# Multiplying 128 tail tokens in the last joint layer instead of in the sweep of batch 1

## The chip, the cores and the metric

One Trainium2 chip, one core. The metric is the device time of one execution of the program, in microseconds. Engines are named as in the profile: PE (TensorE matmul), PEld (its weight load), DVE (VectorE), ACT (ScalarE), POOL (GpSimd), SP (SyncE, which issues most transfers).

## What is computed

Attention over 4 batches, 12 heads, 448 tokens and head size 64, with RMS-normalised q and k, then two feed-forward blocks over all 4 x 448 = 1792 tokens of width 768. In short:

```
x = softmax(scale * norm(q) @ norm(k).T) @ v            # (4, 12, 448, 64) -> (1792, 768)
x = sigmoid(x @ w_gate) * (x @ w_val) @ w_out           # 768 -> 1536 -> 768
h = relu(x @ w_in); out = (h * h) @ w_out2              # 768 -> 2048 -> 768
```

q, k, v and the output are float32, the weights float64. The kernel holds each operand as two fp32r parts (a rounded high part and the rest), and one product of two operands is three matmuls: high x high, high x low and low x high.

## The kernel before

The work has three stages on PE. In `sweep(0)` and `sweep(1)` the four layers of batch 0 and of batch 1 are multiplied one after the other (gate and value, output of the first block, the third layer with relu and square, the last layer). In `joint()` batches 2 and 3 go through the four layers together.

While PE multiplies batch 0, the attention of batch 1 is woven between its matmuls, and while it multiplies batch 1, the attention of batches 2 and 3. Each `yield` in `sweep` is a step. At each step the main loop at the end of the program takes the next slots of the list `slots_of` and emits their work. In sweep 1 there are 204 steps and 202 slots, and one pair of heads takes 16 or 17 slots: scores (`s_mm2`, 4 matmuls into one `att` tile), their maximum (`s_max2`, DVE), the exponentials (`s_exp2`, ACT), the transposes of the result (`c_mm2`, 7 into one `att` tile), the high part of them (`c_hi`, ACT) and the rest (`c_lo`, DVE), the weighted sum of values (`pv_mm2`, 7 matmuls `att<-parts,vs`), and for the next pair the transposes of q and k (`do_a2`, 8 matmuls `att<-ident,qk`) with their split (`a_hi` on ACT, `a_lo` on DVE). There are two `att` tiles in PSUM, used in turn, so each of these steps on PE needs what the last but one left there to have been read. On PE the order in sweep 1 and in `joint` is that of the program (`fixed`). On ACT, DVE, POOL and SP a scheduler sets the order.

Weights come as blocks of 128x768. `next_block` hands out the next and splits the one that is three blocks ahead into a high part (ACT, `wsp<-wraw`) and the rest (DVE). In the last layer of a sweep a block holds 2 of 16 groups of 128 inner rows for half of the 768 columns, and each chunk of 128 tokens takes 6 matmuls of 384 columns per block. 448 tokens are three chunks of 128 and a tail of 64. The third-layer results of the tail of batch 0 are kept in SBUF (`rtail`) in two parts, those of batch 1 join them, and sweep 1 multiplies four chunks: the joined tail `rt` and three of batch 1 (`rb`).

In `joint` every layer is in seven-product form: a product of 2x2 blocks takes seven products in place of eight, with sums and differences of blocks made beforehand (weights in DRAM by accumulating transfers, tokens by DVE in `make`). In its last layer the 896 tokens of batches 2 and 3 are seven chunks of 128. Six of them are in the form (two halves of 384 tokens), and the seventh, `plain`, is multiplied in the plain way by `thin`. Each of the seven products `n` runs over four groups `g`. In each, one weight block is split and 3 x 6 matmuls follow, and `make(n + 1, g)` prepares the tokens of the next product. `thin` adds 6 matmuls in each group of products 0, 1, 4 and 5, and in product 4 a block of weights of its own.

Of the kernel before, what the change touches and what calls it, by code (L numbers as in the profile page):

```python
# [8 lines left out]
F32 = mybir.dt.float32  # L9
# [8 lines left out]
def attention_moe_moe2_kernel(  # L18
# [14 lines left out]
    nc = tc.nc  # L33
# [94 lines left out]
    for both in (((None, (0, 0)),), ((None, (1, 0)),), ((0, None),), ((1, None),), ((2, None), (None, (0, 1))),  # L128
                 ((None, (1, 1)),), ((3, None),)):
# [466 lines left out]
    rtail = {}  # L596

# [146 lines left out]
    def joint():  # L744
# [130 lines left out]
        ra = one.tile([128, 13, 2 * N], F32, tag="hr", name="r")  # L875
        rb = one.tile([128, 3 * 2 * N], F32, tag="pt", name="r")
        plain = one.tile([128, K2, 2, 128], F32R, tag="rt", name="plain")

        def r_of(k):
            return ra[:, k] if k < 13 else rb[:, (k - 13) * 2 * N:(k - 12) * 2 * N]  # L880

        for m2 in range(K2 // 2):
            for m, n, o, sign in seven(yp):
# [4 lines left out]
                if n == 1:  # L888
                    src = r_of(k)[:, 768:896]
                    nc.scalar.copy(out=plain[:, k, 0], in_=src)  # L890
                    nc.vector.tensor_tensor(
                        out=plain[:, k, 1], in0=src, in1=plain[:, k, 0].bitcast(F32), op=ALU.subtract)
        beat_on(30)
        yield
        row0 = 2 * N
        rest = one.tile([128, 7, 2, 384], F32, tag="xy0", name="rest")
        fsum = [rest[:, 3 + i] for i in range(4)]
        dsum = [two.tile([128, 2, 384], F32, tag="qk", name="dsum"), one.tile([128, 2, 384], F32, tag="vs", name="dsum")]
        keep = [rest[:, i // 2, i % 2] for i in range(6)]
        base, third = keep[0:3], keep[3:6]  # L900

        def pairs_of(k, c0, g):
            return [r_of(4 * g + 2 * i + k)[:, c0:c0 + 384] for i in range(2)]

        def vector2(dst, g, in0, in1, op):
            for i in range(2):
                held(nc.vector.tensor_tensor(
                    out=dst[:, i], in0=in0[i] if isinstance(in0, list) else in0[:, i],
                    in1=in1[i] if isinstance(in1, list) else in1[:, i], op=op))

        bufs = [[], []]
        for tag, pool, n in (("raw64", raw_p, 1), ("raw64", raw_p, 1), ("raw64", raw_p, 1), ("qs", one, 1)):
            rp = pool.tile([128, 2, 2, 384], F32R, tag=tag, name="rp")
            bufs[0].append((rp[:, 0], rp[:, 1]))
        xy = one.tile([128, 3, 2, 2, 384], F32R, tag="xy1", name="rp")
        bufs[1] = [(xy[:, i, 0], xy[:, i, 1]) for i in range(3)] + [
            tuple(p_p.tile([128, 2, 384], F32R, tag="p", name="rp") for _ in range(2))]

        def make(n, g):
            dst = bufs[n % 2][g]  # L920
            a11, a12 = pairs_of(0, 0, g), pairs_of(1, 0, g)
            a21, a22 = pairs_of(0, 384, g), pairs_of(1, 384, g)
            if n in (0, 1, 6):
                src = (a11, a12, None, None, None, None, a22)[n]
            elif n == 2:
                vector2(fsum[g], g, a21, a22, ALU.subtract)
                src = fsum[g]
            elif n == 3:
                vector2(fsum[g], g, a11, fsum[g], ALU.subtract)
                src = fsum[g]  # L930
            elif n == 4:
                src = dsum[g % 2]
                vector2(src, g, a11, a21, ALU.subtract)
            else:
                vector2(fsum[g], g, a12, fsum[g], ALU.subtract)
                src = fsum[g]
            if isinstance(src, list):
                for i in range(2):
                    nc.scalar.copy(out=dst[0][:, i], in_=src[i])
                    nc.vector.tensor_tensor(  # L940
                        out=dst[1][:, i], in0=src[i], in1=dst[0][:, i].bitcast(F32), op=ALU.subtract)
            else:
                nc.scalar.copy(out=dst[0], in_=src)
                nc.vector.tensor_tensor(out=dst[1], in0=src, in1=dst[0].bitcast(F32), op=ALU.subtract)
            return dst

        def put(chunk, hf, fn):
            ob = tmp("ob")[:, :384]
            fn(ob)
            row = row0 + 128 * chunk  # L950
            nc.sync.dma_start(out=out[row:row + 128, hf * 384:(hf + 1) * 384], in_=ob)

        xs = [acc_tile()[:, :384] for _ in range(3)]
        y0, y1 = att_tile(), att_tile()
        ys = [y0[:, 0, :384], y0[:, 1, :384], y1[:, 0, :384]]
        zs = [y1[:, 1, :384], acc_tile()[:, :384]]
        bank = [xs, xs, ys, xs, xs, ys, xs]
        ready = {(0, g): make(0, g) for g in range(K4 // 2)}

        def thin(z, wb, g, odd, start, stop):  # L960
            for kk in range(2):
                k = 2 * (2 * g + kk) + odd
                wh, wl = wb[:, 0, kk], wb[:, 1, kk]
                rh, rl = plain[:, k, 0], plain[:, k, 1]
                mm(out=z, lhsT=rh, rhs=wh, start=start and g == 0 and kk == 0, stop=False)
                mm(out=z, lhsT=rh, rhs=wl, start=False, stop=False)
                mm(out=z, lhsT=rl, rhs=wh, start=False, stop=stop and g == K4 // 2 - 1 and kk == 1)

        def end(n, p):
# [8 lines left out]
            elif n == 4:  # L978
                put(p + 3, 1, lambda ob: nc.vector.tensor_tensor(out=ob, in0=third[p], in1=o, op=ALU.subtract))
# [3 lines left out]
            elif n == 6:  # L983
                put(p + 3, 0, lambda ob: nc.vector.tensor_tensor(out=ob, in0=o, in1=base[p], op=ALU.add))

        for n in range(7):
            for g in range(K4 // 2):
# [4 lines left out]
                for p in range(3):  # L992
                    o = bank[n][p]
                    for kk in range(2):
                        rh, rl = (op[i][:, kk, 128 * p:128 * (p + 1)] for i in range(2))
# [5 lines left out]
                    if g == K4 // 2 - 1 and (n != 5 or p > 0):  # L1001
                        if n == 5 and p == 1:
                            end(n, 0)
                        end(n, p)
                if n in (0, 1):
                    thin(zs[0], wb, g, n, n == 0, n == 1)
                elif n == 4:
# [3 lines left out]
            if n in (1, 5):  # L1011
                z = zs[n // 5]
                put(6, n // 5, lambda ob: nc.scalar.copy(out=ob, in_=z))
        yield

    def sweep(s):
# [59 lines left out]
        if s % 2 == 0:  # L1076
            rtail[0] = one.tile([128, 2, K2, 128], F32R, tag="rt", name="rt")
            parts = [(rb, 0, 0, NM), (rtail[0], 0, NM, TAIL)]
        else:
            parts = [(rtail[0], TAIL, 0, TAIL), (rb, 0, TAIL, NM)]  # L1080
# [401 lines left out]
```

## Time and profile before

| | us |
|---|---|
| median of 3 runs (1230.23 to 1231.26) | 1230.28 |
| the profiled execution | 1230.38 |
| its span, from the first to the last instruction | 1228.2 |
| PE busy in the span | 1216.1 |
| PEld busy | 1072.2 |
| DVE busy | 981.8 |
| ACT busy | 797.2 |
| POOL busy | 237.1 |

The profiled execution took 2.2 us more than its span. PE idle is the difference of span and busy time, 12.1 us. The granted clock of PE is full in every slice of the span.

### The profile page before, as it was taken

The numbers are of one execution on the slowest core, as the hardware profiler recorded it, in microseconds if no ns is written. First come the engines' busy times: TensorE is split into PE (matmuls) and PEld (weight loads), VectorE is DVE, ScalarE is ACT, GpSimd is POOL, SyncE is SP. The second block draws the span as 40 slices with busy tenths as digits, with TensorE's granted clock in tenths as the row PEclk, the third lists the DMA queues.
The fourth block names the chain that finished last, engine by engine and source line by source line (L and its number), as shares of the span: only waits on it lengthen the run. The fifth ranks groups of instructions, "written<-read, shape, count | busy, mean of one in ns | idle before, by whom it ended". The sixth has DMA issues, their size and how long they took to land.

```text
span 1228.2 us, 19243 instructions
## 1 busy us (share of the span) xinstructions
PE 1216.1 (99%) x6572; PEld 1072.2 (87%) x6572; DVE 981.8 (80%) x1548; ACT 797.2 (65%) x1611; POOL 237.1 (19%) x248
## 2 busy tenths in 40 slices
PE   8999999999999999999999999999999999999998
PEld 5548878878889988989898999999999999999998
DVE  6888988778975788888788777878888658778793
ACT  6787888667765778876798766765657324335461
POOL 3312222211120113233222220022111112120000
PEclk9999999999999999999999999999999999999999
DMA  5557998888896667787778643597768767675443
GB/s 140 134 162 243 313 293 262 275 256 249 251 316 184 159 161 165 181 177 186 166 183 174 153 93 108 149 210 207 194 179 193 182 166 196 173 194 154 135 148 103
DMA packets 207121, 232.30 MB, mean 189 GB/s; under 512 B 84784, under 2 KB 186288, under 8 KB 207024
## 3 DMA queue, kind: packets, MB, share of 16 engines
q1 hardware_dynamic: 181840, 179.49, 50.4%
q0 software_dynamic: 23296, 51.13, 19.5%
q8 instruction: 52, 0.85, 0.3%
q10 hardware_dynamic: 1888, 0.46, 0.2%
q14 instruction: 45, 0.37, 0.1%
HBM read 192.48 MB, written 81.00 MB: 223 GB/s over the span
## 4 chain that ended last, share of the span: by engine, by line
PE 94%; ACT 2%; DVE 1%; DMA 1%; SPq 1%; issue 1%; ACTq 0%; DVEq 0%
PE acc L578 60%; PE att L578 21%; PE att L583 3%; PE att L303 3%; PE att L357 2%; PE acc L357 1%; PE att L339 1%; PE acc L583 1%; PE acc L339 1%; ACT p L321 1%; DMA ks<-ks 0%; ACT p L470 0%; DMA wraw<-w 0%; PE att L362 0%; DMA qk<-in_k_dram 0%
## 5 line engine op out<-in xcount | busy, mean ns | idle before, releaser
L205 ACT CAST wsp<-wraw 128x768 fp32r<-128x768 f32 x254 | 212.4, 837 | 187.1 <-PE att L578 86.9
L578 PE MATMUL acc<-xy,wsp 128*128 128x448 f32 x1422 | 313.5, 371 | 0.8 <-ACT rl L1093 0.6
L206 DVE TENSOR_TENSOR wsp<-wraw,wsp 128x768 fp32r<-128x768 f32 x254 | 243.3, 959 | 78.0 <-ACT wsp L205 75.1
L578 PEld LDWEIGHTS acc<-xy,wsp 128*128 128x128 f32 x1422 | 261.3, 188 | 31.2 <-issue 6.8
L578 PE MATMUL att<-parts,wsp 128*128 128x448 f32 x828 | 175.8, 365 | 0.0
L578 PEld LDWEIGHTS att<-parts,wsp 128*128 128x128 f32 x828 | 155.5, 188 | 12.3
L578 PE MATMUL acc<-parts,wsp 128*128 128x448 f32 x567 | 122.0, 365 | 0.0
L273 POOL TENSOR_TENSOR ms<-ms,mhalf 112x16 f32<-112x16 f32 (+1 forms) x25 | 79.8, 3195 | 182.8 <-DVE ms L272 182.8
L578 PEld LDWEIGHTS acc<-parts,wsp 128*128 128x128 f32 x567 | 106.4, 188 | 8.4
L578 PE MATMUL acc<-wsp,rb 128*128 128x384 f32 x576 | 108.7, 338 | 0.0
L578 PEld LDWEIGHTS acc<-wsp,rb 128*128 128x128 f32 x576 | 99.8, 188 | 2.3 <-issue 2.0
L578 PE MATMUL acc<-hb,wsp 128*128 128x448 f32 x432 | 95.3, 371 | 0.0
L578 PEld LDWEIGHTS acc<-hb,wsp 128*128 128x128 f32 x432 | 79.3, 188 | 9.4 <-issue 2.7
L177 ACT ACTIVATE wraw<-raw 128x768 f32<-128x768 f32 x67 | 61.1, 917 | 31.2 <-DVE wsp L206 17.9
L192 POOL DMA_DIRECT2D w<-wraw x67 | 37.1, 554 | 219.8 <-DVE wraw L185 195.0
L470 ACT ACTIVATE p<-att,nm 112x448 f32<-112x448 f32 x96 | 60.1, 631 | 17.7 <-DVE nm L459 16.7
L321 ACT ACTIVATE p<-att,nm 112x448 f32<-112x448 f32 x88 | 55.3, 638 | 18.2 <-DVE nm L309 16.5
L185 DVE SCALAR_TENSOR_TENSOR wraw<-wraw,raw 128x768 int32<-128x768 int32 x67 | 63.9, 956 | 1.0
L578 PE MATMUL acc<-wsp,rp 128*128 128x384 f32 x360 | 64.5, 334 | 0.0
L578 PEld LDWEIGHTS acc<-wsp,rp 128*128 128x128 f32 x360 | 62.6, 188 | 0.0
L309 DVE TENSOR_REDUCE nm<-att 112x2 f32<-112x896 f32 x48 | 51.9, 1083 | 8.2 <-PE att L303 8.0
L609 POOL DMA_DIRECT2D wt<-w x32 | 26.6, 909 | 145.2 <-DMA wt<-wt 102.6
(224 smaller groups left out, 2050.8 us busy)
## 6 DMA issues: line engine op xcount, KB each, us to landing
wraw<-w SPq DMA_DIRECT2D x68, 384.0 KB, 3.5
w<-wraw POOLq DMA_DIRECT2D x67, 384.0 KB, 6.1
wraw<-w SPq DMA_DIRECT2D x113, 192.0 KB, 2.9
raw<-in_moe_w_out_dram SPq DMA_DIRECT2D x22, 768.0 KB, 6.3
raw<-in_moe_w_in_dram SPq DMA_DIRECT2D x16, 768.0 KB, 6.2
raw<-in_moe_w_gate_dram SPq DMA_DIRECT2D x12, 768.0 KB, 7.1
raw<-in_moe_w_val_dram SPq DMA_DIRECT2D x12, 768.0 KB, 7.1
ws<-w POOLq DMA_DIRECT2D x48, 192.0 KB, 4.7
```

Of the source, the lines that this page charges most:

```text
L177: size = nc.scalar.activation(out=t, in_=hi.bitcast(F32), func=AF.Prelu, scale=2.0 ** -112, alpha=2.0 ** 32)
L185: nc.vector.scalar_tensor_tensor(out=ti, in0=ti, scalar=3, in1=hi, op0=ALU.logical_shift_left, op1=ALU.bitwise_or)
L192: nc.gpsimd.dma_start(out=w32[i], in_=wraw[i])
L205: nc.scalar.copy(out=sp[:, 0], in_=t)
L206: nc.vector.tensor_tensor(out=sp[:, 1], in0=t, in1=sp[:, 0].bitcast(F32), op=ALU.subtract)
L273: nc.gpsimd.tensor_tensor(out=ms, in0=ms, in1=mhalf[:QR, 0:ms.shape[1]], op=ALU.pow)
L309: nc.vector.tensor_reduce(out=nm, in_=st["s", c][:QR, :, :S], axis=AX.X, op=ALU.max, negate=True)
L321: nc.scalar.activation(out=p[:, e], in_=ps[:QR, e, :S], func=AF.Exp, bias=nm[:, e:e + 1], scale=st["rq"][:, c, e:e + 1] if "rq" in st else ...
L357: nc.tensor.matmul(out=o[e * D:(e + 1) * D], lhsT=v[:, kc, e], rhs=pt[:, (NF + 1) * e + kc if kc < NF else NF], start=(kc == 0), stop=(kc ...
L470: nc.scalar.activation(out=p[:, i * S:(i + 1) * S], in_=ps[:QR, i, :S], func=AF.Exp, bias=nm[:, i:i + 1], accum_out=su[:, c, e:e + 1])
L578: m = latest[0] = nc.tensor.matmul(**kw)
L583: m = nc.tensor.transpose(*a)
```

## The change

Sweep 1 no longer multiplies the joined tail. Both sweeps keep the square of their 64 tail tokens as plain float32 in `rtail`; at the end of the third layer of sweep 1 the whole of it (128 x 2048 floats, 1 MB) is written to a tensor `tails` in DRAM. In `joint`, where the third-layer results of batches 2 and 3 are held in `ra` and `rb`, each row gets 1024 columns in place of 896, and two transfers put `tails` into the last 128. So the last joint layer has 8 chunks, all in seven-product form: two halves of 512 tokens, 4 x 6 matmuls per group in each of the seven products. `thin`, `plain` and the extra weight blocks of product 4 are gone. `make` works on 1024 columns in one instruction where two of 384 stood. The buffers of that stage are laid out anew. In sweep 1 the last layer has the same number of steps, now of 6 matmuls each (before 9, 9 and 6), and from step 156 on a slot comes one step later (`at_step`). The parts of batch 2 and 3 (`x_part`) are now attached to slots.

```diff
-    for both in (..., ((2, None), (None, (0, 1))), ((None, (1, 1)),), ((3, None),)):
+    for both in (..., ((2, None),), ((None, (1, 1)),), ((3, None),)):
...
+    tails = dram_p.tile([128, K2 * 128], F32, tag="tails", name="tails")
...
-        ra = one.tile([128, 13, 2 * N], F32, tag="hr", name="r")
-        rb = one.tile([128, 3 * 2 * N], F32, tag="pt", name="r")
-        plain = one.tile([128, K2, 2, 128], F32R, tag="rt", name="plain")
+        ra = one.tile([128, 12, 1024], F32, tag="hr", name="r")
+        rb = one.tile([128, 4, 1024], F32, tag="rt", name="r")
+        held(nc.sync.dma_start(out=ra[:, :, 2 * N:], in_=from_tails[:, 0:12]))
+        held(nc.sync.dma_start(out=rb[:, :, 2 * N:], in_=from_tails[:, 12:16]))
...
+            hi, lo = room[n % 2][g]
+            a11, a12 = pair_of(0, 0, g), pair_of(1, 0, g)
+            a21, a22 = pair_of(0, 512, g), pair_of(1, 512, g)
...
+                src = dsum if n == 4 else fsum[g]
+                first, second = {2: (a21, a22), 3: (a11, src), 4: (a11, a21), 5: (a12, src)}[n]
+                held(nc.vector.tensor_tensor(out=src, in0=first, in1=second, op=ALU.subtract))
+            nc.scalar.copy(out=hi, in_=src)
+            nc.vector.tensor_tensor(out=lo, in0=src, in1=hi.bitcast(F32), op=ALU.subtract)
...
-                for p in range(3):
+                for p in range(4):
...
-                if n in (0, 1):
-                    thin(zs[0], wb, g, n, n == 0, n == 1)
-                elif n == 4:
-                    thin(zs[1], block(), g, 0, True, False)
-                elif n == 5:
-                    thin(zs[1], wb, g, 1, False, True)
... (sweep)
-                for dst, d0, c0, cn in parts:
-                    low.tensor_tensor(...)
+                low.tensor_tensor(
+                    out=rb[:, 1, m], in0=r2[:, c0:c0 + NM], in1=rb[:, 0, m].bitcast(F32), op=ALU.subtract)
...
-            chunks = [(rtail.pop(0), 0, t0 - TAIL)] + chunks
+            nc.sync.dma_start(out=tails, in_=rtail.pop(0).rearrange("p k n -> p (k n)"))
...
-                        if s == 1 and (c, kk) in ((1, 0), (2, 1)):
+                        if s == 1 and (c, kk) in ((0, 1), (1, 1)):
... (main loop)
+    def at_step(i, total):
+        i += 1
+        if i <= 156:
+            return i + i * 0 // 156
+        return 156 + 0 + (i - 156) * (total - 156 - 0) // 47
```

On PE at the start of the last layer of sweep 1, from the first scores there to those that follow two steps of attention later, this stood before (`rt` is the joined tail, `rb` are the chunks of batch 1, `ks,qs` scores, `ident,p` transposes, `ident,qk` the transposes of `do_a2`, `parts,vs` weighted sums):

```order
L578 MATMUL att<-ks,qs 112x448 x4
L583 MATMUL att<-ident,p 128x112 x7
L578 MATMUL acc<-wsp,rb 128x384 x6
L578 MATMUL acc<-wsp,rt 128x384 x6
L578 MATMUL acc<-wsp,rb 128x384 x3
L583 MATMUL att<-ident,qk 128x112 x8
L578 MATMUL acc<-wsp,rb 128x384 x9
L578 MATMUL att<-parts,vs 128x448 x7
L578 MATMUL acc<-wsp,rb 128x384 x6
L578 MATMUL acc<-wsp,rt 128x384 x6
L578 MATMUL acc<-wsp,rb 128x384 x3
L578 MATMUL att<-ks,qs 112x448 x4
```

and this stands there now:

```order
L577 MATMUL att<-ks,qs 112x448 x4
L582 MATMUL att<-ident,p 128x112 x7
L577 MATMUL acc<-wsp,rb 128x384 x12
L582 MATMUL att<-ident,qk 128x112 x8
L577 MATMUL acc<-wsp,rb 128x384 x6
L577 MATMUL att<-parts,vs 128x448 x7
L577 MATMUL acc<-wsp,rb 128x384 x12
L577 MATMUL att<-ks,qs 112x448 x4
```

The attention on PE is the same, and 15, 9 and 15 matmuls of the layer between its pieces have become 12, 6 and 12. On ACT, a little later in the same layer, from the copies of one `x_part` to those of the next, this stood before (`p` are exponentials, two for one pair of score tiles, `parts<-att` with L491 and L494 the high part of the transposes):

```order
L651 CAST parts<-xwhole 128x448 x2
L470 ACTIVATE p,su<-att,nm 112x448 x2
L491 CAST parts<-att 128x3x224
L494 CAST parts<-att 64x112 x2
L205 CAST wsp<-wraw 128x768
L651 CAST parts<-xwhole 128x448 x2
```

and this stands there now:

```order
L651 CAST parts<-xwhole 128x448 x2
L204 CAST wsp<-wraw 128x768
L490 CAST parts<-att 128x3x224
L493 CAST parts<-att 64x112 x2
L469 ACTIVATE p,su<-att,nm 112x448 x2
L651 CAST parts<-xwhole 128x448 x2
```

The exponentials have moved behind the three copies of the transposes, which come later on PE than the scores that the exponentials read.

## Rows read from the trace of the kernel before

**Rows 1.** Page, part 4: the chain that ended last, by engine.
```profile
PE 94%; ACT 2%; DVE 1%; DMA 1%; SPq 1%; issue 1%; ACTq 0%; DVEq 0%
```

**Rows 2.** Windows, all engines: stretch, length, busy time and instructions, clock, DMA.
```profile
560.00:687.50 127.50, 126.68 (x702) 114.14 (x701) 107.00 (x186) 103.21 (x240) 31.48 (x28) 1.00 0.75 177
687.50:782.50 95.00, 94.65 (x572) 91.28 (x572) 73.42 (x123) 62.34 (x140) 13.82 (x10) 1.00 0.41 107
782.50:1120.30 337.80, 337.80 (x1670) 313.05 (x1669) 266.78 (x397) 166.81 (x289) 61.75 (x75) 1.00 0.75 189
1120.30:1228.20 107.90, 104.22 (x602) 103.89 (x600) 77.31 (x122) 45.45 (x68) 0.82 (x1) 1.00 0.43 130
```

**Rows 3.** Groups of instructions by form, PE: busy us, mean ns, idle before.
```profile
L578 PE MATMUL acc<-wsp,rt 128*128 128x384 f32 x96 | 19.8, 341 | 0.0
L578 PE MATMUL att<-wsp,plain 128*128 128x384 f32 x48 | 9.6, 334 | 0.0
```

**Rows 4.** Timeline, PE, last joint layer: start us, length us, instructions.
```profile
1123.48 1.20 PE L578 MATMUL att<-wsp,plain 128*128 128x384 f32 x6
1124.52 3.28 PE L578 MATMUL acc<-wsp,rp 128*128 128x384 f32 x18
```

**Rows 5.** Timeline, last layer of sweep 1, first pair of heads there.
```profile
691.47 0.83 PE L583 MATMUL att<-ident,p 112*128 112x112 f32 x7
692.08 1.29 PE L578 MATMUL acc<-wsp,rb 128*128 128x384 f32 x6
...
692.96 0.51 ACT L494 CAST parts<-att 64x112 fp32r<-64x112 f32 x2
...
693.49 0.64 ACT L470 ACTIVATE p<-att,nm 112x448 f32<-112x448 f32 x1
...
694.63 0.20 ACT L470 ACTIVATION_READ_ACCUMULATOR p<-att,nm 112x1 f32 x1
...
694.88 0.98 PE L583 MATMUL att<-ident,qk 112*128 112x112 f32 x8
...
700.24 0.63 DVE L437 TENSOR_TENSOR ks<-att,ks 64x448 fp32r<-64x448 f32 x1
...
701.34 0.99 PE L578 MATMUL att<-ks,qs 128*112 128x448 f32 x4
```

**Rows 6.** Timeline, the same layer, second pair of heads.
```profile
717.19 0.62 DVE L536 TENSOR_TENSOR xwhole<-xwhole,att 128x448 f32<-128x448 f32 x1
...
718.10 0.84 PE L583 MATMUL att<-ident,p 112*128 112x112 f32 x7
...
719.64 4.57 POOL L273 TENSOR_TENSOR ms<-ms,mhalf 112x16 f32<-112x16 f32 x1 [10.57 <-DVE ms L272]
...
722.20 0.56 DVE L503 TENSOR_TENSOR parts<-att,parts 64x112 fp32r<-64x112 f32 x2
...
723.76 0.83 PE L583 MATMUL att<-ident,p 112*128 112x112 f32 x7
...
728.09 0.99 PE L583 MATMUL att<-ident,qk 112*128 112x112 f32 x8 [0.35 <-ACT p L470]
```

**Rows 7.** Timeline, the same layer, weighted sum of the second pair.
```profile
746.97 1.73 PE L578 MATMUL att<-parts,vs 128*128 128x448 f32 x7
...
747.18 0.56 DVE L503 TENSOR_TENSOR parts<-att,parts 64x112 fp32r<-64x112 f32 x2
```

**Rows 8.** Windows, products 2 and 3 of the last joint layer with the start of 4.
```profile
1153.60:1187.00 33.40, 33.40 (x195) 33.40 (x194) 30.91 (x49) 18.73 (x26) 0.00 (x0) 1.00 0.45 145
```

**Rows 9.** Groups by form, DVE, 687.5 to 782.5: split of a weight block.
```profile
L206 DVE TENSOR_TENSOR wsp<-wraw,wsp 128x768 fp32r<-128x768 f32 x16 | 15.3, 954 | 3.2 <-ACT wsp L205 3.0
```

**Rows 10.** Page, part 6: transfers, KB each, us to landing.
```profile
raw<-in_moe_w_out_dram SPq DMA_DIRECT2D x22, 768.0 KB, 6.3
```

More of the change, by code (lines that the diff above doesn't have):

```diff
@@ L897, in joint @@
[L897 to L917, printed above, removed]
+        xy0 = one.tile([128, 5, 1024], F32R, tag="xy0", name="rp")
@@ new lines, in joint @@
+        xy1 = one.tile([128, 5, 1024], F32R, tag="xy1", name="rp")
+        pt = one.tile([128, 3, 1024], F32R, tag="pt", name="rp")
+        raw = [raw_p.tile([128, 1536], F32R, tag="raw64", name="rp")[:, :1024] for _ in range(3)]
+        kqs = [two.tile([128, 1024], F32, tag="kq", name="sums") for _ in range(2)]
+        qst = one.tile([128, 1024], F32, tag="qs", name="sums")
+        qks = [two.tile([128, 1024], F32, tag="qk", name="sums") for _ in range(2)]
+        vst = one.tile([128, 2, 512], F32, tag="vs", name="keep")
@@ new lines, in by_k @@
+        def by_k(t):
+            return t.rearrange("p (k n) -> p k n", k=2)
+        room = [
+            [(pt[:, 0], pt[:, 1]), (pt[:, 2], raw[0]), (raw[1], raw[2]), (xy0[:, 4], xy1[:, 4])],
+            [(t[:, i], t[:, i + 1]) for t in (xy1, xy0) for i in (0, 2)]]
+        room = [[(by_k(a), by_k(b)) for a, b in half_] for half_ in room]
+        fsum = [by_k(t) for t in (kqs[0], kqs[1], qks[0], qst)]
+        dsum = by_k(qks[1])
+        pkeep = [p_p.tile([128, 2, 384], F32, tag="p", name="keep") for _ in range(3)]
@@ L919, in make, with pair_of @@
+        keep = [t[:, i] for t in pkeep for i in range(2)] + [vst[:, i, :384] for i in range(2)]
+        base, third = keep[0:4], keep[4:8]
+        def pair_of(k, c0, g):
+            t, k0 = (ra, 4 * g + k) if g < 3 else (rb, k)
+            return t[:, k0:k0 + 3:2, c0:c0 + 512]
         def make(n, g):
-            dst = bufs[n % 2][g]
-            a11, a12 = pairs_of(0, 0, g), pairs_of(1, 0, g)
-            a21, a22 = pairs_of(0, 384, g), pairs_of(1, 384, g)
+            hi, lo = room[n % 2][g]
+            a11, a12 = pair_of(0, 0, g), pair_of(1, 0, g)
+            a21, a22 = pair_of(0, 512, g), pair_of(1, 512, g)
@@ L949, in put @@
             fn(ob)
-            row = row0 + 128 * chunk
+            row = 2 * N + 128 * chunk if chunk < 7 else N - TAIL
             nc.sync.dma_start(out=out[row:row + 128, hf * 384:(hf + 1) * 384], in_=ob)
[L953 to L956, printed above, removed]
+        xs = [acc_tile()[:, :384] for _ in range(4)]
+        ys = [t[:, i, :384] for t in (att_tile(), att_tile()) for i in range(2)]
         bank = [xs, xs, ys, xs, xs, ys, xs]
         ready = {(0, g): make(0, g) for g in range(K4 // 2)}
[L960 to L967, printed above, removed]
         def end(n, p):
@@ L978, in end @@
             elif n == 4:
-                put(p + 3, 1, lambda ob: nc.vector.tensor_tensor(out=ob, in0=third[p], in1=o, op=ALU.subtract))
+                put(p + 4, 1, lambda ob: nc.vector.tensor_tensor(out=ob, in0=third[p], in1=o, op=ALU.subtract))
                 nc.vector.tensor_tensor(out=base[p], in0=base[p], in1=o, op=ALU.add)
@@ L983, in end @@
             elif n == 6:
-                put(p + 3, 0, lambda ob: nc.vector.tensor_tensor(out=ob, in0=o, in1=base[p], op=ALU.add))
+                put(p + 4, 0, lambda ob: nc.vector.tensor_tensor(out=ob, in0=o, in1=base[p], op=ALU.add))
         for n in range(7):
@@ L1000, in joint @@
                         mm(out=o, lhsT=rl, rhs=wh, start=False, stop=g == K4 // 2 - 1 and kk == 1)
[L1001 to L1004, printed above, removed]
-                if n in (0, 1):
-                    thin(zs[0], wb, g, n, n == 0, n == 1)
-                elif n == 4:
-                    thin(zs[1], block(), g, 0, True, False)
-                elif n == 5:
-                    thin(zs[1], wb, g, 1, False, True)
-            if n in (1, 5):
-                z = zs[n // 5]
-                put(6, n // 5, lambda ob: nc.scalar.copy(out=ob, in_=z))
+                    if g == K4 // 2 - 1:
+                        if n != 5:
+                            end(n, p)
+                        elif p % 2:
+                            end(n, p - 1)
+                            end(n, p)
         yield
@@ L1425, in attention_moe_moe2_kernel @@
         total, done = len(slots), 0
-        extra = steps_of_1() if s == 1 else {}
+        extra = steps_of_1(slots) if s == 1 else {}
         for i, _ in enumerate(sweep(s)):
@@ L1436, in attention_moe_moe2_kernel @@
                 fn(*args)
[L1437 removed]
+            want = min(total, at_step(i, total) if s == 1 else (i + 1) * total // 66)
             while done < want:
```

67 lines of the change are left out of this document (19 added, 48 removed).

## The prediction

> **What bounds the kernel now.** The chain that ended last comes first: 94% of it is PE [rows 1]. So nearly all of the time is matmuls issued one after the other, and a change pays by the matmuls that it removes, less the waits that it makes on PE. The busy time by stretch says where such waits could come up [rows 2]. In the joint layers PE is busy for all of the 337.80 us, and in the last layer of sweep 1 (687.5 to 782.5) for 94.65 of 95.00 us. What differs is how close the others are. In that last layer DVE is busy for 73.42 us, 77%, and ACT for 62.34; in the layers ahead of it, with the same attention between their matmuls, DVE has 107.00 of 127.50 us, 84%. These shares are only averages: what PE waits for in such a layer are chains from PE over DVE and ACT back to PE, and whether they end in time is read from single places of the timeline, below.
>
> **Matmuls.** The tail chunk took 96 matmuls in sweep 1 [rows 3], and `thin` another 96 in the joint layer (two banks, of which the rows show the first; 2 halves x 16 groups x 3). The joint layer had 7 products x 4 groups x 18 = 504 besides, and now has 7 x 4 x 24 = 672. So 96 go in sweep 1, and 672 - 504 - 96 = 72 are added in the joint layer: 24 fewer in all. Six matmuls of 384 columns follow each other in 1124.52 - 1123.48 = 1.04 us [rows 4], 0.1733 us each. That is -16.64 us in sweep 1 and +12.48 us in the joint layer, together -4.16 us.
>
> **The waits in sweep 1.** The last layer of sweep 1 keeps its attention, and has 288 matmuls between its pieces where 384 stood. PE's work there falls to 94.65 - 16.64 = 78.0 us, DVE's stays at about 73 us: 94% if PE never waited. For each piece of attention on PE I take the time from its start back to the end of the chain that it needs, which is its slack, and set against it the matmuls that leave the stretch.
>
> *Two `att` tiles, exponentials.* After the transposes that start at 691.47 ACT makes their high part (until 693.47) and then the exponentials of the scores before them, the last of which is read out by 694.83; the transposes of q and k start at 694.88 [rows 5]. From the start of the transposes the chain is 3.36 us long, and PE has 0.61 us of transposes (691.47 to 692.08) and 15 matmuls, 2.60 us. It arrives with almost nothing to spare. With 12 matmuls PE needs 2.69 us and waits 0.67 us. The order of ACT now puts the exponentials behind the copies before the next pair's first scores too, where they stood ahead, with again 12 matmuls in front, and the second `ident,qk` gets 12 in place of 18: it waits already, 0.35 us [rows 6]. Three places, 2.0 us.
>
> *Scores behind `do_a2`.* They need `a_lo`, which ends at 700.24 + 0.63 = 700.87; they start at 701.34 [rows 5], slack 0.47. Since the chain starts at `ident,qk`, all 6 matmuls count that leave between (24 to 18), 1.04 us: 0.57 us, in two pairs 1.1 us.
>
> *Transposes.* Those at 718.10 need a sum on DVE that ends at 717.81 [rows 6], slack 0.29; 3 matmuls (0.52) leave: 0.2 us. Those at 723.76 need `c_lo`, which ends at 722.76, slack 1.0; 6 leave, 1.04, and a maximum now stands ahead of `c_lo` on DVE: between 0.04 and about 1, I take 0.5.
>
> *Weighted sum.* The one at 746.97 starts while `c_lo` still runs, until 747.74 [rows 7]; no slack, 6 matmuls leave: 1.0 us.
>
> These add up to 4.9 us, and for the last pair, whose pieces I find with 1 us of slack or more, I add 0.1: 5.0 us. Against the 0.35 us of PE idle time that the layer has now, that is +4.65. From below: without the terms that rest on a new order of ACT or DVE (0.67 and 0.5), and if ACT and DVE, which catch up in each wait, halve the rest, 1.9 us. From above: DVE is nowhere in sweep 1 kept busier than the 84% of the layers ahead [rows 2]; at that share its 73.4 us take 87.5 us, a wait of 9.5 us. The mid value is that of single places, which is what I trust. The second `ident,qk` could cost up to 1.2 us more than counted, as the power on POOL that it needs took 4.57 us [rows 6].
>
> [...] PEld is busy for 91.28 of the 95.00 us here, 96% [rows 2]. [...]
>
> **What costs nothing.** *The last joint layer:* an instruction on DVE takes 0.63 us for 448 columns [rows 5] and 0.954 for 768 [rows 9], so about 1.21 for 1024 and 0.57 for 384. In product 3 DVE then has 4 splits of weights (3.8), 4 differences and 4 rests of 1024 (9.7) and 8 sums at the end (4.6): 18.1 us for 96 matmuls, 16.6 us. That is over by 1.5 us. Before, product 3 had 3.8 + 3.8 + 8 x 0.57 + 6 x 0.57 = 15.6 us for 72 matmuls, 12.5 us, over by 3.1, and PE stood busy in all of its stretch [rows 8]: `make` runs about one product ahead. I take 0, and 3 us (products 3 and 4) if that lead is gone. *The round trip of the tail:* 768 KB take 6.3 us to land [rows 10], so 1 MB some 8.4 us each way. The write stands on SP between weight loads of sweep 1. The read waits for the last matmul on `h`, and the next weight loads stand behind it. Blocks are split three ahead, and one of the joint layers is 18 matmuls of 337.80 / 1670 = 0.202 us [rows 2], 3.64 us: a lead of 10.9 us covers 8.4. `make` first reads the new columns in product 2's sums, 100 us later. If the cover fails, it costs up to the 8.4; I take 0. *Smaller work:* 32 rests of 64 columns in sweeps 0 and 1, and the 16 copies and 16 rests of `plain`, leave ACT and DVE, where PE doesn't wait for them; four weight blocks fewer. I take 0 for the rest of the sweeps, and at most 0.6 us of gain, for which PE idles in the layers ahead of the last, 127.50 - 126.68 = 0.82 us [rows 2].
>
> **Sum:** -16.64 + 12.48 + 4.65 = +0.49 us on the profiled execution's 1230.38 us, whose span is 1228.2 us; the median of the runs shown, 1230.28, is 0.1 us off, nothing here. So 1230.9 us. What a measurement of this kernel tells from no change is about 0.2%, 2.46 us.
>
> **The rivals.**
> *The waits are hidden, the matmuls pay.* DVE idles for 21.6 of the 95.00 us, and in a layer with more slots per us it would only use them; ACT and DVE lose the small work of the third layer. Waits of 0 to 1.7 us give -4.5 to -2.8 us, 1225.9 to 1227.6. Against it stand three places without any slack [rows 5 to 7]. Chance 26%.
> *DVE becomes the bound of the last layer of sweep 1: slower.* Every piece of attention passes through DVE in order, so one late instruction delays the next chain too, and PE would go at DVE's pace. If DVE stays at the 84% that it has in the layers ahead, the layer takes 87.5 us: 87.5 - 95.0 + 12.5 = +5.0, 1235.4 us. It decides from waits of 7 us on (+2.5). Against it: ACT, which shared the load there (103.21 of 127.50), has less here. Chance 20%.
> *The lead in the last joint layer is lost*, or the read of the tail holds up weights: +3 us and more on the sum, 1233.9. Against it, the rows above. Chance 4%.
>
> **How the numbers follow.** The forecast, waits between 2.0 and 6.9 us and so 1228.0 to 1232.8, has 50%. Faster by over 0.2% (under 1227.8) is the first rival, 0.26; slower the other two, 0.24. The range takes in the forecast, half of the first rival and most of the second: 1226.9 to 1234.6 leaves out some 0.12 below and 0.07 above.
>
> **What would show it.** In the profile after, the last layer of sweep 1 should take about 83 us with 78 us of PE busy, and PE's waits there be for `p` (ACT L469) at the `att` transposes and for DVE L436, L498 and L502 at scores and weighted sums, each of 0.2 to 1 us. The last joint layer should have 672 matmuls at 0.1733 us without idle time between them, 12.5 us longer. I am wrong in the size of the waits if that layer takes 79 us or 87; in the cover if PE idles at 1010 to 1030 us or between products 3 and 5.

## The result and the profile after

The changed kernel took 1240.7 us (median of 7 executions, 1235.58 to 1246.09), the kernel before, run beside it, 1231.26 (1230.18 to 1231.76). The ratio is 1.0074, with a 95% interval of 1.0056 to 1.0092: slower by 9 us, where 1230.9 was forecast and 1234.6 was the upper end of the range. The executions also lie nearly seven times as far apart as before. The profiled one took 1237.03 us, with a span of 1235.2, so the profile shows some 7 of the 9 us.

The chain that ended last [rows 1] has lost PE and holds ACT, DVE and DMA now:

```profile
PE 87%; ACT 5%; DVE 3%; DMA 3%; issue 1%; SPq 1%; ACTq 0%; DVEq 0%
```

The busy time by stretch after, for the stretches of [rows 2]:

```profile
565.00:693.00 128.00, 127.24 (x704) 114.75 (x704) 105.12 (x171) 103.61 (x240) 31.52 (x28) 1.00 0.75 176
693.00:777.50 84.50, 79.92 (x480) 74.53 (x479) 70.44 (x118) 61.07 (x138) 12.24 (x10) 1.00 0.46 124
777.50:1115.10 337.60, 337.60 (x1669) 312.73 (x1667) 267.08 (x384) 162.69 (x270) 61.56 (x75) 1.00 0.76 193
1115.10:1235.20 120.10, 116.64 (x673) 116.32 (x671) 87.50 (x99) 46.30 (x54) 1.30 (x2) 0.99 0.36 107
```

The last layer of sweep 1 takes 84.5 us in place of 95, the last joint layer 120.1 in place of 107.9, and the joint layers between them are the same. That is what the forecast spoke of. But the last layer of sweep 1 starts at 693.0 and not at 687.5. Cut by the start of each stage on PE, the two profiles compare like this (us):

| stage | before | after | difference | forecast |
|---|---|---|---|---|
| start-up and sweep 0 up to its last layer | 332.24 | 332.86 | +0.62 | 0 |
| last layer of sweep 0 | 66.25 | 71.15 | **+4.90** | 0 |
| sweep 1 up to its last layer | 289.03 | 289.00 | -0.03 | 0 |
| last layer of sweep 1 | 95.28 | 84.47 | -10.81 | -11.99 |
| three joint layers | 337.55 | 337.59 | +0.04 | 0 |
| last joint layer | 107.85 | 120.18 | +12.33 | +12.48 |
| span | 1228.20 | 1235.24 | +7.04 | +0.49 |

5.5 of the 7.0 us stand in sweep 0, in which not one matmul was added or taken away. PE's share of 350 to 400 us there, first before, then after (columns: stretch, length, PE busy and instructions, clock, DMA share, GB/s):

```profile
350.00:400.00 50.00, 50.00 (x298) 1.00 0.75 230
```

```profile
350.00:400.00 50.00, 46.01 (x274) 1.00 0.71 222
```

The timeline of the kernel before at the place, SP's queue (from 345 us on) and ACT:

```profile
346.06 9.33 SPq L154 DMA_DIRECT2D raw<-in_moe_w_out_dram  x3
356.79 1.20 SPq L403 DMA_DIRECT2D v<-in_v_dram  x2
...
364.56 0.62 ACT L412 CAST vs<-v 128x512 fp32r<-128x512 f32 x1 [0.95 <-DMA v<-in_v_dram]
365.08 0.53 ACT L348 COPY pt<-att 128x448 f32<-128x448 f32 x1
```

and after:

```profile
347.91 11.67 SPq L153 DMA_DIRECT2D raw<-in_moe_w_out_dram  x4
359.67 0.95 SPq L402 DMA_DIRECT2D v<-in_v_dram  x2
...
368.77 0.62 ACT L411 CAST vs<-v 128x512 fp32r<-128x512 f32 x1 [4.32 <-DMA v<-in_v_dram]
369.30 0.90 ACT L176 ACTIVATE wraw<-raw 128x768 f32<-128x768 f32 x1
370.10 0.52 ACT L347 COPY pt<-att 128x448 f32<-128x448 f32 x1
...
371.01 1.01 PE L302 MATMUL att<-kq 64*112 64x448 f32 x4 [1.29 <-ACT pt L348]
...
377.97 0.98 PE L582 MATMUL att<-ident,qk 112*128 112x112 f32 x8 [2.45 <-ACT p L320]
```

`vs<-v` is the high part of the values of the first pair of sweep 1. It is wanted much later, but it stands in ACT's order in the last layer of sweep 0, before as after. On SP four loads of raw weights now go ahead of the load of v where three did, counted from 345 us. So v is issued 2.9 us later and has landed 4.3 us later (at 368.75, before at 364.46). ACT stands for 4.32 us where it stood for 0.95, and behind it stand the copies of the transposes, the weights and the exponentials that PE needs. Only 16 instructions had left sweep 0, the rests of 64 columns on DVE: with them gone, the scheduler chose another order on PE, ACT, DVE and SP.

Below, "at full clock" is said of executions with a mean granted clock of 0.998 or more, while a median with a ratio is of all executions, also of those (25 of 101 of the kernel before) that took 3 to 7 us longer at a mean granted clock of 0.993 to 0.997.

### The profile page after: what moved, and what is told of

Its sections match the earlier page's. It is cut to its first block, busy times and chain, and to the rows that moved or that the text cites. A ratio compares the mean times of both kernels' runs of the same rounds, so it can differ in the third digit from the quotient of the medians.

```text
span 1235.2 us, 19055 instructions
## 1 busy us (share of the span) xinstructions
PE 1214.3 (98%) x6548; PEld 1067.5 (86%) x6548; DVE 985.1 (80%) x1475; ACT 792.4 (64%) x1576; POOL 235.6 (19%) x248
## 4 chain that ended last, share of the span: by engine, by line
PE 87%; ACT 5%; DVE 3%; DMA 3%; issue 1%; SPq 1%; ACTq 0%; DVEq 0%
PE acc L577 54%; PE att L577 21%; PE att L582 3%; PE att L302 2%; PE att L356 2%; PE acc L356 1%; ACT p L320 1%; PE acc L582 1%; PE att L338 1%; PE acc L338 1%; DMA raw<-in_moe_w_gate_dram 1%; ACT wraw L176 1%; DMA v<-in_v_dram 1%; DMA raw<-in_moe_w_val_dram 1%; ACT p L469 1%
## 5 line engine op out<-in xcount | busy, mean ns | idle before, releaser
L204 ACT CAST wsp<-wraw 128x768 fp32r<-128x768 f32 x250 | 208.8, 836 | 205.7 <-PE att L577 104.8
L205 DVE TENSOR_TENSOR wsp<-wraw,wsp 128x768 fp32r<-128x768 f32 x250 | 239.5, 959 | 73.6 <-ACT wsp L204 71.0
L577 PE MATMUL acc<-wsp,rp 128*128 128x384 f32 x480 | 83.7, 334 | 0.0
L577 PEld LDWEIGHTS acc<-wsp,rp 128*128 128x128 f32 x480 | 83.3, 188 | 0.0
L308 DVE TENSOR_REDUCE nm<-att 112x2 f32<-112x896 f32 x48 | 51.9, 1083 | 8.6 <-PE att L302 8.2
L458 DVE TENSOR_REDUCE nm<-att 112x2 f32<-112x896 f32 x48 | 52.1, 1085 | 3.2 <-PE att L577 2.5
```

Of the source, the lines that this page charges most:

```text
L204: nc.scalar.copy(out=sp[:, 0], in_=t)
L205: nc.vector.tensor_tensor(out=sp[:, 1], in0=t, in1=sp[:, 0].bitcast(F32), op=ALU.subtract)
L308: nc.vector.tensor_reduce(out=nm, in_=st["s", c][:QR, :, :S], axis=AX.X, op=ALU.max, negate=True)
L458: nc.vector.tensor_reduce(out=nm, in_=st["s", e, c2][:QR, :, :S], axis=AX.X, op=ALU.max, negate=True)
L577: m = latest[0] = nc.tensor.matmul(**kw)
```

## The experiments

### Is it the order of sweep 0?

Three kernels on one chip: `a_rest0` puts the 16 rests of sweep 0 back, `b_norest0` takes them out of the kernel before (and sets their place to zero once), and `a_again` is the changed kernel again.

```diff
 a_rest0 (on the changed kernel, third layer)
+                if s == 0:
+                    low.tensor_tensor(
+                        out=rtail[0][:, 1, m, 0:TAIL], in0=r2[:, d0:d0 + TAIL], in1=dst, op=ALU.subtract)
 b_norest0 (on the kernel before)
-                for dst, d0, c0, cn in parts:
+                for dst, d0, c0, cn in parts[:1] if s == 0 else parts:
                     low.tensor_tensor(
```

Expected of a_rest0:

> The changed kernel with the 16 rests of 64 columns put back on DVE in the third layer of sweep 0 (written to a part of rtail that nobody reads). With them the order on PE, ACT, DVE, SP and POOL in sweep 0 is that of the kernel before, word for word. Theory A (the loss is the new order of sweep 0, in which ACT stands behind the transfer of v): the last layer of sweep 1 starts at 687.5 us instead of 693.0, and the time is 1230.5 to 1232 us with a spread of under 3 us. Rival B (the tensor tails in DRAM and its transfers delay others): still 1236 to 1246 us, and the spread stays. Rival C (the waits in the last layer of sweep 1 differ from run to run): the start is at 687.5, but the median stays over 1235 us.

Expected of b_norest0:

> The kernel before without the 16 rests of batch 0's tail on DVE in sweep 0 (that part is set to zero once, so the tail of batch 0 loses its low part); nothing else of the change. The order of sweep 0 on PE, ACT, DVE and SP is then that of the changed kernel. Theory A: it loses as the changed kernel does, 1235 to 1241 us, runs 5 us or more apart, and the last layer of sweep 1 starts near 693 us. Rivals B and C: 1231 us, the start at 687.5 us.

Expected of a_again:

> The changed kernel as it is, for a second trace beside those two: 1236 to 1246 us. Theory A: what differs between the two traces of it stands before 693 us, in waits of PE for what ACT does behind a transfer of v or raw. Rival C: it stands in the last layer of sweep 1.

In the traces the order of sweep 0 on all engines is that of the kernel before in a_rest0, and that of the changed kernel in b_norest0, but for one memset on POOL. PE from 350 to 400 us in a_rest0, then in b_norest0, then in a_again:

```profile
350.00:400.00 50.00, 50.00 (x298) 1.00 0.74 227
```

```profile
350.00:400.00 50.00, 45.07 (x269) 1.00 0.69 220
```

```profile
350.00:400.00 50.00, 46.47 (x268) 0.97 0.69 220
```

ACT in b_norest0:

```profile
368.69 0.62 ACT L412 CAST vs<-v 128x512 fp32r<-128x512 f32 x1 [4.71 <-DMA v<-in_v_dram]
```

The cross is clean. The kernel before without 16 small subtractions loses what the changed kernel loses (last layer of sweep 0: 72.11 us), at 1236.22 us, ratio 1.0045 (1.0028 to 1.0062). The changed kernel with 16 subtractions for nobody takes 66.25 us there, as before, with the tensor `tails` and its transfers in place. In a_again the granted clock is 0.50 from 377.8 to 381.2 us, after PE's idle time from 374.3 to 376.7 (2.42 us), and the 44 matmuls from 377.55 on take 8.78 us where b_norest0 has 7.21: this gap cost twice. In the profile of after a gap of 2.45 us left the clock at full (1.00).

But a_rest0, at 1234.18 us, ratio 1.0031 (1.0013 to 1.0049), is not all of the way back (the last layer of sweep 1 starts at 689.0 us, not at 687.5, behind a wait for ks of 1.61 us), and it went against my number of 1230.5 to 1232 with a small spread. Its lowest execution took 1231.63; two at full clock took 1238.50 and 1239.53, and the latter is the profiled one. The time is in the joint layers, where nothing waits. First 900 to 1000 us of a_again, then of a_rest0:

```profile
900.00:1000.00 100.00, 100.00 (x495) 1.00 0.77 190
```

```profile
900.00:1000.00 100.00, 100.00 (x485) 1.00 0.73 183
```

The same matmuls of 448 columns come 206.6 ns apart (start to start, mean of the single starts) instead of 202.7, at a granted clock of 1.00, until the last joint layer begins: 1660 x 3.9 ns = 6.5 us. The joint layers take 344.12 us, not 337.55. That was new to me.

### Is it ACT behind the transfer of v?

`a_vheld` ties that one copy to its place in the program. With it the rest of v (DVE) and four loads of the next v (SP) leave the last layer of sweep 0; the other instructions of sweep 0 keep the new order.

```diff
+        first = nc.scalar.copy(out=vs[:, :, 0::3], in_=t)
+        if (st["b"], st["hp"]) == (2, 0):
+            held(first)
```

> The changed kernel with one tie: the high part of v of the first pair of sweep 1 (the copy on ACT to which the 4.32 us of idle time in sweep 0 belong) is scheduled behind the matmul that precedes it in the program, so it leaves the last layer of sweep 0. The other work of ACT there keeps the new order. Theory A1 (ACT standing behind the transfer of v is the loss in sweep 0): PE is busy for 49.5 to 50 us of 350 to 400, the last layer of sweep 1 starts at 687.5 to 689.5 us, the time falls by 4 to 6 us to 1232 to 1234. Rival A2 (the whole new order with its raw loads is slower): PE still loses 2 us or more between 350 and 400 and the time stays over 1235.

PE from 350 to 400 us:

```profile
350.00:400.00 50.00, 49.70 (x297) 1.00 0.71 227
```

The last layer of sweep 0 falls to 67.13 us, so the copy behind v's transfer is 4.0 of the 4.9 us lost there. The total, 1235.61 us, fell by less than forecast: in its profile sweep 1 up to the last layer took 3.7 us more, with waits for `ks` of 1.37 and 0.37 us and, behind the first, 3.4 us at a clock of 0.50, and two executions at full clock (1238.69, 1242.46) are 5 us and more over its lowest, 1232.9.

### What sets the slower pace of the joint layers?

In after, a_again, a_rest0 and a_vheld one matmul at the start of the joint layers comes 13 to 39 ns late, always the 27th. In a_rest0 the slower pace begins there. The one ahead of it, the 26th (of which the expectations speak), reads the rest of T1 of the last column block, which DVE ends only 0.12 us (after) to 0.16 us (a_rest0) before it starts. DVE in after; the 26th matmul starts at 782.66:

```profile
781.91 0.62 DVE L654 TENSOR_TENSOR parts<-t,parts 128x448 fp32r<-128x448 f32 x1
```

In the kernel before the same rest ends at 785.75 for a matmul that starts at 787.98. What waits is the matmul's weight load (PEld), first in after, then in the kernel before:

```profile
782.59 0.19 PEld L577 LDWEIGHTS att<-parts,wsp 128*128 128x128 f32 x1
```

```profile
787.78 0.19 PEld L578 LDWEIGHTS att<-parts,wsp 128*128 128x128 f32 x1
```

Before, the load starts 200 ns ahead of its matmul, as all loads around it do (195 to 205 ns). In after it starts 53 ns behind the end of the rest, which leaves 71 ns of that lead (77 to 105 ns in a_again, a_rest0, a_vheld and a_rest01, of which below). The layer ahead is 10.8 us shorter now, and DVE has not become faster by that. I took the late result for the cause (theory P) and moved the rest to both sides. `a_t1` puts it earlier, `b_t1late` puts it late in the kernel before.

```diff
 a_t1 (on a_rest0): the next sum is scheduled behind the rest of T1
+        if j == 2:
+            behind(add_t2, rest[0])
 b_t1late (on the kernel before): the rest of T1 behind that of T4
+    tc.add_manual_dep(rests["T1", 2].ins, rests["T4", 2].ins.name, ...)
```

> The changed kernel with the 16 rests in sweep 0 (order of the kernel before) and, on DVE, the rest of T1 of the last column block put ahead of the next two sums, 1.1 us earlier. In the profiles of the changed kernel the 26th matmul of the joint layers waits 10 to 40 ns for that rest, and in one profile all 1586 matmuls of 448 columns after it stand 206.6 ns apart in place of 202.7, 6.6 us in all. Theory P (that small wait is what throws the matmuls into the slower pace in some executions): no execution with a full clock is over 1234 us, the median is 1231.0 to 1232.5. Rival: the slower pace has another cause and comes as before in 2 or 3 of 12 executions, at 1237 to 1240 us with a full clock.

> The kernel before with that rest of T1 put behind the rest of T4 on DVE, so that the 26th matmul of the joint layers waits for it, by the profile before some 0.4 to 0.6 us; nothing else. Theory P: besides the 0.5 us (1231.3) some of the executions take 1236 to 1239 us at a full clock, and a profile of such a one shows 206.6 ns in the joint layers. Rival: 1231.3 us in all, 202.7 ns. If a longer wait sets the pace again in the same way each time, all executions are alike, at either level.

Neither has an execution at full clock that is 5 us over its lowest (6 and 10 of them, 1232.61 to 1234.36 and 1230.43 to 1234.67 us). Both have a longer wait instead, 0.55 us for T2 in a_t1 (1234.58 us, ratio 1.0032, 1.0020 to 1.0044) and 0.56 us for T1 in b_t1late (1231.92, 1.0009, 0.9997 to 1.0020), and it costs little more than itself (the joint layers of b_t1late take 338.22 us, 0.67 more). The median that I gave for a_t1, 1231.0 to 1232.5, was missed, and b_t1late went against theory P as it stood, which wanted some executions at 1236 to 1239. So it isn't any wait. `b_hiccup` makes it a short one, with nothing else of the change:

```diff
 b_hiccup (on the kernel before)
+        if j == 2:
+            rests["again"] = nc.vector.tensor_tensor(out=t4, in0=t2, in1=b21, op=ALU.subtract)
+            held(rests["again"])
...
+    tc.add_manual_dep(rests["T1", 2].ins, rests["again"].ins.name, ...)
```

> The kernel before with the rest of T1 of the last column block moved back on DVE behind four others and one sum made twice (0.53 us more on DVE), so that by the profile of b_t1late it ends 20 to 40 ns after the 26th matmul of the joint layers asks for it; in b_t1late it was 0.56 us late, and no execution was in the slower pace. Nothing else of the change is in it. Theory P (a wait of some 30 ns throws the matmuls of 448 columns into 206.6 ns): as in the kernels with that wait (9 of 37 executions at full clock were 5 us or more over their lowest) 1 to 4 of about 10 executions at full clock are at 1236 to 1239 us, the others at 1230 to 1232. Rival (the slower pace comes with the change's buffers or transfers): all at 1230 to 1233.

Its profile has the 26th matmul 24 ns late, and stayed at 202.7 ns. Of 7 executions at full clock five took 1230.87 to 1232.25 and two 1237.88 and 1238.18, while the 15 of the kernel before beside it took 1231.55 at most. No profile fell on one of the two; that they go at 206.6 ns is inferred from their time, some 6 us over the median of the five. The median of all is 1235.1, ratio 1.0029 (1.0010 to 1.0048), but it lies between two levels; at full clock the mean is 1233.5 against 1230.8, so a wait of 24 ns costs the kernel before some 2.7 us.

Executions at full clock that are 5 us or more over the lowest of their kernel:

| by the profile | executions | 5 us or more over |
|---|---|---|
| result 0.12 to 0.16 us ahead of its matmul: after 3 of 6, a_again 0 of 4, a_rest0 2 of 8, a_vheld 2 of 9, a_rest01 2 of 10 | 37 | 9 |
| b_hiccup, 24 ns too late | 7 | 2 |
| a_best (below), 0.18 us ahead | 8 | 3 |
| early enough, or late by 0.5 us and more: b_norest0, a_t1, b_t1late, a_k4, a_t1s, a_pv | 43 | 0 |
| the kernel before, beside the experiments | 76 | 0 |

On each of the four chips of the experiments the difference shows by itself. The profiles that show the slower pace are two, those of a_rest0 and a_rest01; for the other executions it is inferred from the time.

### What is left with the order restored

`a_rest01` puts the 32 rests of both sweeps back, so that the order is that of before up to the last layer of sweep 1 (in a_rest0 one transfer of k still stood behind a sum of weights on SP, and the scores at 645 us waited 1.61 us for ks). `a_t1s` makes T1 at slot 200, which needs no result of the last pair of heads.

```diff
 a_t1s (on a_rest01)
+        slots[200].insert(0, lambda: x_part(2, "sums"))
```

> The changed kernel with all 32 rests of the tail back on DVE, in sweep 0 and sweep 1 (nobody reads them). With them the order on ACT, DVE and SP is that of the kernel before up to the last layer of sweep 1; in the kernel a_rest0 one transfer of k still stood behind a weight sum on SP in sweep 1, and the scores at 645 us waited 1.6 us for ks. If the loss outside the two stages that the change is about is only the order that the scheduler made: the stretches before the last layer of sweep 1 take what they took before (687.5 us), no wait for ks at 645 us, the last layer 84.4 us, the last joint layer 120.2 us, so 1.5 us over the kernel before: 1232.0 to 1232.6 us for executions at full clock. If the transfer of ks is late by chance or through the tensor tails: up to 1.5 us more.

> The kernel a_rest01 with the first of the four sums of the last column block (T1, which needs no result of the last pair of heads) made at slot 200 instead of after the last slot. The 26th matmul of the joint layers then has no wait, and the other sums come 1.1 us earlier too. Theory P (the wait of 10 to 40 ns there throws the matmuls of 448 columns from 202.7 to 206.6 ns in some executions): no execution at full clock is over 1235 us, the fastest are those of a_rest01. Rival: 2 of 12 are at 1238 to 1240 us at full clock, as in a_rest0.

a_rest01: 1232.66 us, ratio 1.0012 (0.9996 to 1.0028). Its stages are 332.33, 66.25, 289.78, 84.47, 344.13 (the slower pace, after a 27th matmul 31 ns late) and 120.14 us. Two executions are at 1237.65 and 1238.91, the other eight at full clock at 1231.61 to 1235.11, and the median of the ten is 1232.26, as expected. a_t1s: 1233.71, ratio 1.0019 (1.0004 to 1.0034); at full clock none over 1234.36, as theory P wants, the median of these 1232.6. The matmul that reads T2 is late by 0.68 us there now (0.55 in a_t1), so it isn't faster.

### The waits in the last layer of sweep 1

The waits of PE there, after. The first seven answer to the places of [rows 5 to 7], the eighth is of the last pair:

```profile
700.37 0.99 PE L582 MATMUL att<-ident,qk 112*128 112x112 f32 x8 [0.47 <-ACT p L469]
706.51 1.03 PE L577 MATMUL att<-ks,qs 128*112 128x448 f32 x4 [0.56 <-DVE ks L436]
712.02 1.07 PE L577 MATMUL att<-ks,qs 128*112 128x448 f32 x4 [0.66 <-ACT p L469]
721.91 0.86 PE L582 MATMUL att<-ident,p 112*128 112x112 f32 x7 [0.22 <-DVE xwhole L535]
730.29 0.98 PE L582 MATMUL att<-ident,qk 112*128 112x112 f32 x8 [0.45 <-ACT p L469]
736.42 1.04 PE L577 MATMUL att<-ks,qs 128*112 128x448 f32 x4 [0.55 <-DVE ks L436]
748.24 1.70 PE L577 MATMUL att<-parts,vs 128*128 128x448 f32 x7 [1.25 <-ACT p L469]
774.42 1.48 PE L577 MATMUL att<-parts,vs 128*128 128x448 f32 x6 [0.17 <-DVE parts L498]
```

`a_k4` (on a_t1) moves four slots out of the layer, `a_pv` (on a_t1s) gives the first weighted sum of each pair the accumulator that the fourth chunk has left free, `a_best` (on a_pv) puts weight copies on ACT behind the exponentials and the rest of T2 ahead of others.

```diff
 a_k4 (on a_t1)
+            return i + i * 4 // 156
+        return 156 + 4 + (i - 156) * (total - 156 - 4) // 47
 a_pv
+            spare[0] = acc_tile() if s == 1 else None
...
+        if e == 0 and spare[0] is not None:
+            o, rt = spare[0][:, :S], None
 a_best
+        if spare[0] is not None and exps:
+            for i in made:
+                behind(i, exps[-1])
```

> The kernel a_t1 with four slots of attention moved ahead out of the last layer of sweep 1 (up to step 156 one slot more every 39 steps, and four steps of the last layer without one). If the eight waits of PE there are of slots that stand too close for ACT and DVE, four steps of 6 matmuls (1.04 us each) without a slot take 1.5 to 3 us of the 5.8 us, and the layers ahead lose under 1 us: 1229 to 1230.5 us. If ACT and DVE are the bound in the layers ahead (84% busy on DVE there), they lose as much: 1231 to 1233.

> The kernel a_t1s with the first weighted sum of each pair, in the last layer of sweep 1, put into the accumulator that three chunks leave free there, so that it needs no att tile. If the waits of that layer are of the turn of the two att tiles: the wait of 1.25 us before a weighted sum goes, and of the 0.45 to 0.65 us waits before transposes of q and k and scores that name the exponentials most go too; the layer takes 81.5 to 82.5 us in place of 84.4, and the time falls by 2 to 3 us to 1229.5 to 1230.5. If they are of ACT's and DVE's own pace, the layer stays at 83.8 us or more and the waits turn up at the next pieces.

> The kernel a_pv with two ties more. In the last layer of sweep 1 the high part of a weight block (ACT) stands behind the exponentials of the same step, not ahead of them, where in a_pv it waited for its buffer while they stood behind it, and PE for them for 1.25 us. At the start of the joint layers the rest of T2 goes ahead of T4 and of the rest of B22 on DVE, which takes the 0.55 us wait there. If both hold: 1.2 to 1.9 us less than a_pv, 1229.4 to 1230.2 us, under the kernel before by 0.1%. If the exponentials are late for another reason, DVE's maximum above all: 1231 us as a_pv.

a_k4 took 1237.59 us, ratio 1.0044 (1.0028 to 1.0060), 1234.83 at full clock, where a_t1 has 1233.78. The layer falls to 78.42 us, but the layers ahead of it take 298.32 in place of 290.57 (a_t1): more is lost than won. By estimate some 1.6 of these 7.75 us are of 3.4 us at a clock of 0.50 (in a_again such a stretch cost 8.78 - 7.21 = 1.57 us), behind a wait of 1.81 us for the input of transposes (DVE).

a_pv took 1231.27 us, ratio 0.9995 (0.9986 to 1.0004): no difference from the kernel before, and 1.3 us under a_t1s at full clock, where I had given 2 to 3. The layer takes 83.20 us. Its waits, same view:

```profile
695.12 0.99 PE L586 MATMUL att<-ident,qk 112*128 112x112 f32 x8 [0.47 <-ACT p L469]
706.01 1.07 PE L581 MATMUL att<-ks,qs 128*112 128x448 f32 x4 [0.64 <-ACT p L469]
716.19 0.86 PE L586 MATMUL att<-ident,p 112*128 112x112 f32 x7 [0.22 <-DVE xwhole L539]
724.58 0.99 PE L586 MATMUL att<-ident,qk 112*128 112x112 f32 x8 [0.47 <-ACT p L469]
741.74 1.69 PE L581 MATMUL att<-parts,vs 128*128 128x448 f32 x7 [1.25 <-ACT p L469]
767.90 1.48 PE L581 MATMUL att<-parts,vs 128*128 128x448 f32 x6 [0.18 <-DVE parts L498]
```

The two waits for ks are gone. The longest stayed, since it belongs to the second weighted sum, which still takes an `att` tile; I had named the wrong one. a_best missed: 1235.29 us, ratio 1.0027 (1.0009 to 1.0045). The 1.25 us went, and 1.69 us came before the next transposes:

```profile
728.56 0.96 PE L596 MATMUL att<-ident,qk 112*128 112x112 f32 x8 [0.84 <-ACT p L469]
742.32 0.86 PE L596 MATMUL att<-ident,p 112*128 112x112 f32 x7 [1.69 <-DVE parts L502]
```

Its T2 no longer makes PE wait, and ends at 782.60 for a matmul that starts at 782.78. Three of its 8 executions at full clock took 1238.17 to 1239.12, the other five 1231.62 to 1234.8: the short wait again, it seems. In its profile no matmul is late there, but the weight load of the one at 782.78 starts 122 ns ahead of it, where some 200 are usual.

## Why the prediction was wrong

The forecast of 1230.9 us fell at the step "I take 0 for the rest of the sweeps". I had read that 32 rests leave ACT and DVE "where PE doesn't wait for them", and priced the work that left. I had not priced what the scheduler does with the gap. Shown by b_norest0 and a_rest0: the 16 rests of sweep 0 alone move the load of v, and without them the last layer of sweep 0 takes 4.9 us (after) and 5.9 us (b_norest0) more. In the profile that is most of the loss of 7.0 us. A second place of the same kind, the transfer of k in sweep 1, cost 1.6 us in a_rest0 and a_t1 and nothing in the profile of after.

*Matmuls.* -16.64 and +12.48: right. The last joint layer measured +12.33, without idle time.

*Waits in the last layer of sweep 1.* The places were right, and their releasers but for one, and the stage took 84.47 us where 83.3 was forecast. PE's idle time there is 84.50 - 79.92 = 4.6 us, against the 5.0 that I summed: three places of 0.67 measured 0.45, 0.47 and 0.66, the scores 0.56 as forecast, the transposes 0.2 and not 0.7. The weighted sum measured 1.25 against 1.0, and that it came so near is luck: I had it wait for `c_lo`, and it waits for the exponentials on ACT. The end of `c_lo` that I read in [rows 7] is needed only by the seventh matmul of that sum, which starts at 748.33 in the trace of the kernel before. But a wait costs more than the idle time that the view shows. In a_rest0 the transposes at 696.36 start 0.81 us after the matmul before, where 0.175 is usual: 0.64 us lost, and 0.47 shown, since a matmul counts as busy beyond the start of the next (six for 1.20 us, with the next one 1.04 us after the first [rows 4]). Eight waits at some 0.16, where the layer before had one, make 1.1 of the 1.6 us by which the layer is longer than its matmuls and idle time say. The term was mis-sized by 1.2 us.

*The turn of the two `att` tiles* has a part in these waits: with one accumulator more for one of the eleven uses of `att` per pair, in a_pv, 1.3 us of the layer went (83.20 us, where after has 84.47).

*DVE as the bound* didn't come with its size: the layer took 84.5 us, not 87.5. But DVE had 70.44 us of work there, not the 73.4 that I used, and its share is 83%, near the 84% of that rival; it is 83 to 85% in every kernel with the change, also where a wait was moved (a_k4 84, a_pv and a_best 85). So that DVE's pace has a part in these waits is not excluded; no run changes DVE's work there alone. *The weight loads*, had they alone set the layer's time, would have given its 16.64 us back: PEld's busy time there fell by 91.28 - 74.53 = 16.75 us, and the layer by 10.81.

*Last joint layer and the round trip of the tail:* nothing, as forecast. PE is busy in all of 777.5 to 1115.1 us.

*The start of the joint layers* stood in no step. I said that the layer ahead gets shorter and did not ask who had used that time: DVE's parts for the first joint products had 2.2 us of slack and lost nearly all of it. That goes with the slower pace in part of the executions, and in b_hiccup the short wait alone brings executions of that length to the kernel before. The rest of the median's 9 us and the spread I put down to it, together with the stall in sweep 0, but that is inferred: the three long executions of the changed kernel at full clock are 8.2 to 10.5 us over its lowest, more than the 6.5 that the pace costs, and no profile fell on one.

With the order restored, the change costs about what its sum says: a_rest01 is 1.1 us over the kernel before at full clock (1232.26 against 1231.12 beside it), where the sum of the two changed stages is +1.5 and the forecast was +0.5. (The lower end of the forecast, with 2.0 us of waits, is 1227.9 by its own terms, not 1228.0; nothing rests on it.)

## What to carry to other kernels

Where a scheduler sets the order, an instruction that is taken away anywhere is an edit everywhere: compare the order of all engines over the whole program, look for an in-order engine that now stands ahead of a landing transfer, and price that, or tie the order. When a stage gets shorter, take the slack of whatever feeds the next one, since it shrinks too (here by 2.1 of 2.2 us). And where runs of one kernel lie far apart, take profiles until one falls on each level; a median over two levels says little of the edit.

## What the runs showed of the hardware

A wait of some 30 ns went with a loss of 6.6 us (joint layers of 344.12 us in a_rest0 and 344.13 in a_rest01, in place of 337.55). Where a result came 0.12 to 0.16 us before the matmul that reads it, the weight load waited for it and started 71 to 105 ns before the matmul instead of 195 to 205, and the next matmul was 13 to 39 ns late (in b_hiccup, with the result 24 ns too late and a load 2 ns ahead, it was 104). In two of these profiles all matmuls of 448 columns behind it go at 206.6 ns in place of 202.7, up to the last joint layer and without a wait in between; there, with 384 columns (0.1733 us), the pace is the usual one. By their times about a quarter of the executions (14 of 52) did so. Waits of 0.55 us and more there didn't do it in 39 executions. In the usual pace the steps cycle through 199, 203 and 207 ns, and the lead of the weight load through 196, 200 and 204; in the slower one each step is 206 or 207 and nearly each lead 204 or 205. What holds the pace no run shows.

ACT took its instructions in order: in after it stood for 4.32 us until v had landed, at 368.75, and the copy at 370.10 came behind that of v, though the transposes that it reads had ended at 365.62.
